# Moving one of nine small start-up transfers from ScalarE's DMA queue to the sync engine's

## The chip, the cores and the metric

The kernel runs on one core of a Trainium2 chip. The metric is the device time of one execution in microseconds (us). Before the change the median of 8 executions is 555.18 us (554.63 to 556.37). The engines are PE (TensorE: matmuls; PEld is its weight load), ACT (ScalarE), DVE (VectorE), POOL (GpSimd) and SP (the sync engine, which issues DMAs only). ACT can issue DMAs as well; "ACTq" and "SPq" in the profile are such issues.

## The reference, cut to what matters

Two layers, each an attention with a compressive memory followed by a feed-forward part, on 2048 tokens of width 640, with 32 heads of width 20. The sequence is cut into four segments of 512 tokens; within a segment attention is causal softmax, and across segments a memory matrix built from a feature map of the keys is read by the mapped queries.

```
phi = lambda t: jnp.where(t > 0, t + 1.0, jnp.exp(t))
for s in range(N):
    qs, ks, vs = (q[:, :, s].copy(), k[:, :, s].copy(), v[:, :, s].copy())
    logits = jnp.einsum('bhqd,bhkd->bhqk', qs, ks) * scale + mask
    p = _softmax(logits, axis=-1)
    a_dot = jnp.einsum('bhqk,bhkd->bhqd', p, vs)
    pq = phi(qs)
    num = jnp.einsum('bhld,bhde->bhle', pq, M)
    den = jnp.einsum('bhld,bhd->bhl', pq, z)[..., None] + 1e-06
    o = g * (num / den) + (1.0 - g) * a_dot
    pk = phi(ks)
    M = M + jnp.einsum('bhld,bhle->bhde', pk, vs)
    z = z + jnp.einsum('bhld->bhd', pk)
...
x = x + _A_ref(_layernorm(x, axis=-1), A_wq, A_wk, A_wv, A_wo, A_beta)
x = x + _B_ref(_layernorm(x, axis=-1), B_w1, B_w2)
```

The last two lines run twice, with the same weights.

## The kernel before

The program is not written in its final order. Some forty Python generators ("streams") each describe one kind of work: scores, exponentials, causal masks, projections, layer norms, spills to DRAM, fills from DRAM, the feed-forward part, and so on. A greedy planner (`Sched.run`, line 295) asks every stream for its next instruction, works out from hand-written costs when that could start on each engine that may take it, picks the one with the smallest start time (ties go to the smaller priority number), appends it to that engine's list and moves the engine's clock to its end. A stream that waits for an event which no other stream has set yet (`Need`) offers nothing. So the planner's clocks decide the order of all 18,665 instructions, and the chip then runs each engine's list in order, with semaphore waits between them.

The costs that matter here are in the helpers. `act` (line 404) charges 60 ns + n/1.2 for n columns read from PSUM, 94 ns + n/1.2 for others; `dve` (line 399) charges 66 ns + n/(0.96 x mode). `evac` (line 408), an evacuation from PSUM to SBUF, offers both ACT and DVE and takes the one that the planner believes to end first. `dma` (line 417) charges the issuing engine's clock with `issue` and gives a landing time from size and `lat`.

The heads are worked on in pairs of groups: a group is 4 heads (80 rows of the 640 features), and a pair is 8 heads. For the score matmuls, each head's 20 rows of queries and keys must stand at partition 0, 32, 64 or 96 of a buffer called `pad`. The projections leave queries and keys in `stg`, in 5 chunks of 128 feature rows. For all pairs but the first, a chunk goes out to DRAM (`spill`, line 942; its DMA is line 955) and comes back in the padded layout (`fill`, line 989; line 1002), all on SP. For the very first pair of segment 0 the detour is left out: `first_heads` (line 960) copies straight from `stg` to `pad`, one DMA for each head (line 982), z = 0 being the first group and z = 1 the second, hh = 0 to 3 the head in the group. The third head of the second group straddles the border of chunks 0 and 1 and is moved in two pieces (8 and 12 rows). So z = 0 makes 4 DMAs, all on SP, and z = 1 makes 5, all on ACT. Each is planned with `issue=720.0`.

When the last piece of a group is planned, `first_heads` sets the event `pad` of that group. At the end it sets `direct` 0 and 1. Three streams hang on these:

- the scores (`scores`, line 1164; the matmuls are line 1186). A pair goes through five rounds; rounds 0 and 1 read only group z = 0, rounds 2 to 4 read z = 1. The exponentials (line 1248, ACT) follow round by round, two for each.
- `spill` of chunk 1 in segment 0 starts with `Need("direct", 1)`, though its DMA waits only for the evacuations of chunk 1. Chunk 0 isn't spilled; its event `packed` is set with the tickets of `direct` 0, that is with the landing of the last piece of both groups.
- the feature map (`phi_`, line 1010) of a chunk waits for `packed`: DVE line 1029, then ACT line 1031, then DVE line 1032, priority 4.

Other names that the text uses: line 621 loads beta on SP (in `consts`, priority 7), and ACT's line 624 waits for it; line 550 are SP's loads of later tokens (`late_loads`, priority 8); line 734 (DVE) normalises the next segment's tokens (`lnorm`, priority 5), line 710 transposes them by DMA, and the projections of that segment follow (lines 667 and 670 are the two ways in which `group` emits a matmul: whole, or as four of 32 columns; the planner chooses by the mode that PE is in, and charges a change of mode). Lines 866 and 867 are the evacuations of queries and keys on DVE and ACT; line 921 is the evacuation of values on either.

Of the kernel before, what the change touches and what calls it, by code (L numbers as in the profile page):

```python
# [38 lines left out]
class Prog:  # L39
# [44 lines left out]
    def dma(self, e, fn, sem):  # L84
        self.pos[e] += 1
        self.dcnt[id(sem)] = self.dcnt.get(id(sem), 0) + 16
        tk = (sem, self.dcnt[id(sem)])
        self.ops[e].append(("op", fn, sem, 16))
        self.info[(id(sem), tk[1])] = ("dma%d" % id(sem), tk[1], dict(self.K[e]))
        return tk  # L90
# [332 lines left out]
def bass_interleave_layers__memory_aug_infini_attn__dense_activation_relu__prompt_kernel(  # L423
    nc, A_x, A_wq, A_wk, A_wv, A_wo, A_beta, B_x, B_w1, B_w2, out,
):
    with contextlib.ExitStack() as es:
# [533 lines left out]
        def first_heads():  # L960

            sl = yield Acq(PAD)
            sems = pad_sem[id(sl)], sem_("first")
            tks = []
            for z in range(2):
                ev = []
                for n in range(2):
                    t = yield Need("stg", 0, 0, 0, n)
                    ev = ev + t
                sem = sems[z]  # L970
                for hh in range(4):
                    r0 = 80 * z + 20 * hh
                    cuts = [r0, r0 + DH] if r0 // 128 == (r0 + DH - 1) // 128 else [r0, 128, r0 + DH]
                    for ra, rb in zip(cuts, cuts[1:]):
                        c = ra // 128
                        if c == 1 and ra == 128:
                            ev = []
                            for n in range(2):
                                t = yield Need("stg", 0, 0, 1, n)
                                ev = ev + t  # L980
                        p0 = 32 * hh + ra - r0
                        tk = yield dma(("sp", "act")[z], sem, 2048 * (rb - ra), lambda e, p0=p0, ra=ra, rb=rb, c=c, z=z: e.dma_start(  # L982
                            sl.ap[p0:p0 + rb - ra, z], stg[ra - 128 * c:rb - 128 * c, c]), ev + sl.tks, issue=720.0, rate=200.0)
                S.set("pad", 0, 0, z, tks=[sl, tk])
                tks.append(tk)
            S.set("direct", 0, tks=tks)
            S.set("direct", 1, tks=tks[1:])

        def fill(a, s):
            got = []  # L990
            for g in range(0, G, 2):
                if (a, s, g) == (0, 0, 0):
                    yield from first_heads()
                    continue
                sl = yield Acq(PAD)
                w = []
                for c in range(80 * g // 128, (80 * g + 159) // 128 + 1):
                    t = yield Need("packed", a, s, c)
                    w += t
                for hh in range(4):  # L1000
                    src = scr[s % 2, 80 * g:80 * g + 160, :].rearrange("(g h d) t -> d h g t", g=2, d=DH)[:, hh]
                    tk = yield dma("sp", pad_sem[id(sl)], 81920, lambda e, sl=sl, src=src, hh=hh: e.dma_start(  # L1002
                        sl.ap[32 * hh:32 * hh + DH].rearrange("p g n t -> p g (n t)"), src), w + sl.tks, issue=350.0, rate=130.0)
                for z in range(2):
                    S.set("pad", a, s, g + z, tks=[sl, tk])
                got.append(tk)
            S.set("filled", a, s, tks=got)
# [622 lines left out]
```

The softmax here doesn't subtract the row's maximum and nothing guards it: scores larger than these inputs give would overflow.

## Time and profile before

| what | value |
|---|---|
| median of 8 executions | 555.18 us (554.63 to 556.37) |
| the profiled execution, its own time | 555.04 us |
| its span, first to last instruction | 553.3 us |
| granted TensorE clock | 1.000 |
| exponentials, ACT line 1248 | 320, 308.9 us, mean 1027 ns |
| evacuation of 512 columns, ACT line 867 / DVE line 866 | mean 598 / 684 ns |
| evacuation of 320 columns, ACT line 921 / DVE line 921 | mean 441 / 485 ns |
| line 982 on SP | 4, median 718 ns, 13.2 to 15.7 us |
| line 982 on ACT | 5, median 732 ns, 14.6 to 19.3 us |
| beta load, line 621, issue to landing | 2.8 us |

The profile is one execution of the whole program. Times in it run from the first instruction. "Busy" of an engine excludes DMA issues, which the profile shows as the engine's queue. A wait of several semaphores is put down to the one that came last. The difference of 1.7 us between the execution's time and its span lies before the first and after the last instruction.

### The profile page before, as it was taken

To read this page: it belongs to the slowest core of one execution; us is meant where nothing else is said; L and a number is where in the kernel's file an instruction comes from. 1 tells how busy PE (TensorE), PEld (TensorE's weight loads), DVE (VectorE), ACT (ScalarE), POOL (GpSimd) and SP (SyncE) were. 2 spreads that over 40 slices of the span, in tenths; PEclk is the share of its full clock that TensorE was granted. 3 is DMA by queue.
4 is the path that set the end of the run, shared out by engine and by line. 5 is a ranking of instruction groups with operands and counts; after the bars stand their busy time and mean duration, and the time that the engine had idled before them with its cause. 6 is when DMAs were issued, how large, how long until landed. Compare 5 with 4: busy or idle time off the path is not lost.

```text
span 553.3 us, 18665 instructions
## 1 busy us (share of the span) xinstructions
PE 545.1 (99%) x8130; PEld 309.0 (56%) x8130; DVE 412.1 (74%) x1061; ACT 407.3 (74%) x516; POOL 189.7 (34%) x302
## 2 busy tenths in 40 slices
PE   8999999999999999999999999999999999999998
PEld 7454554455564555646456554565555654666756
DVE  5967989898799888897878888769885787335102
ACT  5699889889777987798788887679987678432140
POOL 5346344333344344343433443035331443201000
DMA  8596999935845148256186521872429512354101
GB/s 273 134 235 159 233 181 212 231 65 70 191 92 91 31 101 189 50 98 88 39 184 127 88 45 39 166 153 39 69 61 208 103 30 30 87 84 62 40 2 51
DMA packets 130291, 61.30 MB, mean 111 GB/s; under 512 B 109090, under 2 KB 120098, under 8 KB 130210
## 3 DMA queue, kind: packets, MB, share of 16 engines
q1 hardware_dynamic: 129648, 59.58, 50.7%
q8 instruction: 64, 1.05, 0.8%
q10 hardware_dynamic: 562, 0.53, 0.3%
q14 instruction: 17, 0.14, 0.1%
HBM read 20.57 MB, written 12.85 MB: 60 GB/s over the span
## 4 chain that ended last, share of the span: by engine, by line
PE 94%; ACT 2%; DMA 1%; DVE 1%; SPq 1%; issue 0%; POOL 0%; ACTq 0%; POOLq 0%
PE ps L667 47%; PE ps L670 25%; PE ps L1186 9%; PE ps L1280 6%; PE ps L1066 2%; PE ps L1319 1%; ACT PT L1248 1%; PE ps L1123 1%; PE ps L644 1%; PE ps L1460 1%; DMA pad<-scr 1%; DMA beta_bc<-in_A_beta_dram 1%; SPq L982 0%; ACT stg L867 0%; SPq L1002 0%
## 5 line engine op out<-in xcount | busy, mean ns | idle before, releaser
L1248 ACT ACTIVATE PT<-ps 128x1024 bf16<-128x1024 f32 x320 | 308.9, 1027 | 65.5 <-PE ps L1186 60.1
L1260 POOL TENSOR_SCALAR_AFFINE_SELECT PT<-PT 128x512 bf16<-128x512 bf16 x256 | 163.8, 658 | 264.3 <-ACT PT L1248 264.2
L667 PE MATMUL ps<-w_r,hT 128*128 128x320 bf16 x510 | 82.4, 300 | 0.0
L1506 DVE TENSOR_TENSOR x_sb<-x_sb,ps 128x320 bf16<-128x320 bf16 (+1 forms) x65 | 31.1, 478 | 59.5 <-PE ps L670 44.2
L670 PE MATMUL ps<-xnT,w_r 128*32 128x512 bf16 x1112 | 65.4, 379 | 0.3 <-issue 0.3
L1186 PE MATMUL ps<-pad 20*128 20x512 bf16 (+3 forms) x1024 | 63.4, 301 | 1.5 <-ACT PT L1248 0.9
L667 PEld LDWEIGHTS ps<-w_r,hT 128*128 128x128 bf16 x510 | 47.6, 98 | 24.5 <-issue 6.8
L667 PE MATMUL ps<-xnT,w_r 128*128 128x512 bf16 x242 | 59.8, 380 | 0.0
L688 DVE BATCH_NORM_STATS2 stats<-x_sb 128x6 f32<-128x320 bf16 x124 | 55.8, 474 | 2.6 <-DMA x_sb<-in_A_x_dram 2.2
L1485 ACT ACTIVATE hT<-ps 128x512 bf16<-128x512 f32 x56 | 33.5, 598 | 21.8 <-PE ps L670 20.5
L670 PE MATMUL ps<-w_r,hT 128*32 128x320 bf16 (+1 forms) x1340 | 49.0, 294 | 0.0
L1186 PEld LDWEIGHTS ps<-pad 20*128 20x128 bf16 x1024 | 17.8, 92 | 52.6 <-ACT PT L1248 28.1
L1402 DVE TENSOR_TENSOR x_sb<-x_sb,ps 128x320 bf16<-128x320 bf16 x64 | 30.0, 480 | 18.1 <-PE ps L667 10.2
L670 PEld LDWEIGHTS ps<-xnT,w_r 128*32 128x32 bf16 x1112 | 29.1, 97 | 25.2 <-issue 0.6
L1280 PE MATMUL ps<-PT,v_aug 128*21 128x128 bf16 (+3 forms) x896 | 40.4, 301 | 0.0
L670 PEld LDWEIGHTS ps<-w_r,hT 128*32 128x32 bf16 x1340 | 34.8, 97 | 9.0
L667 PE MATMUL ps<-wo_r,oT 128*128 128x320 bf16 x242 | 38.9, 300 | 0.0
L1290 DVE CAST otu<-ps 128x512 bf16<-128x512 f32 x48 | 32.8, 682 | 7.5 <-PE ps L1280 6.9
L1484 DVE TENSOR_SCALAR hT<-ps 128x512 bf16<-128x512 f32 x48 | 32.7, 682 | 6.4 <-PE ps L667 4.3
L704 POOL TENSOR_TENSOR rstd<-lnU,mhalf 128x2 f32<-128x2 f32 (+2 forms) x26 | 20.6, 791 | 46.0 <-DVE lnU L700 36.1
L667 PEld LDWEIGHTS ps<-xnT,w_r 128*128 128x128 bf16 x242 | 21.7, 97 | 24.5 <-issue 4.6
L866 DVE CAST stg<-ps 128x512 bf16<-128x512 f32 x45 | 30.6, 684 | 5.8 <-PE ps L667 5.6
(109 smaller groups left out, 735.8 us busy)
## 6 DMA issues: line engine op xcount, KB each, us to landing
pad<-scr SPq DMA_DIRECT2D x124, 80.0 KB
scr<-stg SPq DMA_DIRECT2D x34, 256.0 KB, 3.1
out_dram<-x_sb SPq DMA_DIRECT2D x15, 160.0 KB, 1.8
w_r<-in_B_w_dram SPq DMA_DIRECT2D x10, 216.0 KB, 2.6
w_r<-in_B_w_dram SPq DMA_DIRECT2D x13, 160.0 KB, 3.0
x_sb<-in_A_x_dram SPq DMA_DIRECT2D x10, 160.0 KB, 3.3
scr<-w_r SPq DMA_DIRECT2D x5, 256.0 KB, 3.0
wv_r<-in_A_wv_dram SPq DMA_DIRECT2D x1, 800.0 KB, 8.5
```

The costliest lines, as they stand in the source:

```text
L667: return e.matmul(view(dst.ap, b), a, b, start=(k == 0), stop=(k == last))
L670: return e.matmul(view(dst.ap[rows], b), part, b, start=(k == 0), stop=(k == last))
L688: tk = yield dve(320, 1, lambda e, c2=c2: e.bn_stats(stats6[:, t % 12, c2, :], x_sb[:, t, c2 * 320:(c2 + 1) * 320]), xt)
L866: te = yield evac(N, 1, lambda e: e.tensor_copy(sg.ap[:, t0:t0 + N], bk.ap[:, 0:N]), lambda e: e.activation(sg.ap[:, t0:t0 + N], bk.ap[:, ...
L1186: fns.append([(lambda e, z=z, j=j, hh=hh, N=N, o=o, sl=sl, q=hh % 2: e.matmul(slot.ap[:, q, o:o + N], sl.ap[32 * hh:32 * hh + DH, z, 0, 12 ...
L1248: tx = yield act(1024, lambda e, dst=dst, src=src: e.activation(dst, src, ACT.Exp, scale=SCALE), sc + pw)
L1260: tm = yield pool(600.0, lambda e, reg=reg: e.affine_select(out=reg, in_=reg, pattern=[[0, 4], [1, 128]], compare_op=ALU.is_ge, fill=0.0, ...
L1280: fns.append((lambda e, OD, j=j, hh=hh: e.matmul(OD.ap[32 * hh:32 * hh + DH + 1, 128 * j:L], VAUG[vx(a, s)][:, j, 4 * g + hh, :], pt.ap[:, ...
L1290: te = yield evac(L, 1, lambda e: e.tensor_copy(dst, OD.ap), lambda e: e.activation(dst, OD.ap, ACT.Copy), [tk] + OTU[0].tks)
L1484: th = yield evac(512, 1, lambda e: e.tensor_scalar(hT[:, dc, :], bk.ap[:, :], 0.0, None, ALU.max), lambda e: e.activation(hT[:, dc, :], b ...
L1485: lambda e: e.activation(hT[:, dc, :], bk.ap[:, :], ACT.Relu), [tk] + HT.tks)
L1506: ta = yield dve(n, 1, lambda e: e.tensor_tensor(x_sb[:, t, c0:c0 + n], x_sb[:, t, c0:c0 + n], bk.ap[:, 0:n], ALU.add), [tk], urgent=True)
```

## The change

The DMA of the fourth head of the second group (z = 1, hh = 3; 20 rows of 2048 bytes) is issued by SP. The other four pieces of z = 1 stay on ACT. The semaphore, the data and the planned cost are the same.

```diff
                         p0 = 32 * hh + ra - r0
-                        tk = yield dma(("sp", "act")[z], sem, 2048 * (rb - ra), lambda e, p0=p0, ra=ra, rb=rb, c=c, z=z: e.dma_start(
+                        tk = yield dma("act" if z and hh < 3 else "sp", sem, 2048 * (rb - ra), lambda e, p0=p0, ra=ra, rb=rb, c=c, z=z: e.dma_start(
                             sl.ap[p0:p0 + rb - ra, z], stg[ra - 128 * c:rb - 128 * c, c]), ev + sl.tks, issue=720.0, rate=200.0)
```

## The prediction, made before the changed kernel was run

> **What bounds the kernel now.** I read the busy times and the chain that ended last, then stretches of 20 us, then the queues around the change.
>
> ```profile
> PE 545.1 (99%) x8130; PEld 309.0 (56%) x8130; DVE 412.1 (74%) x1061; ACT 407.3 (74%) x516; POOL 189.7 (34%) x302
> PE 94%; ACT 2%; DMA 1%; DVE 1%; SPq 1%; issue 0%; POOL 0%; ACTq 0%; POOLq 0%
> ```
>
> TensorE (PE) is busy for 545.1 of 553.3 us, so 8.2 us is all the time in which it does nothing. The stretches show where those lie (columns: length, PE, PE weight load, DVE, ACT, POOL, clock, DMA share, GB/s):
>
> ```profile
> 0.00:20.00 20.00, 17.62 (x154) 13.86 (x155) 12.41 (x37) 9.89 (x23) 7.32 (x23) 1.00 0.67 204
> 20.00:40.00 20.00, 19.38 (x226) 10.12 (x224) 15.98 (x41) 19.13 (x25) 9.30 (x15) 1.00 0.90 227
> 40.00:60.00 20.00, 18.61 (x310) 9.97 (x311) 16.35 (x46) 19.99 (x22) 11.63 (x18) 1.00 0.70 175
> 60.00:80.00 20.00, 20.00 (x230) 11.86 (x232) 17.23 (x51) 16.03 (x25) 6.61 (x10) 1.00 0.96 213
> 80.00:100.00 20.00, 19.47 (x321) 8.59 (x313) 17.82 (x46) 18.71 (x25) 8.40 (x13) 1.00 0.84 193
> ```
>
> Before 20 us PE lacks 2.38 us, the start-up. From 20 to 60 it lacks 0.62 + 1.39 = 2.01 us, and there ACT works 19.13 and then 19.99 of 20 us: this is the stage in which ACT, not PE, sets the pace. From 80 to 100 PE lacks 0.53. All stretches from 100 to 540 together lack 0.74 (0.08 at 200, 0.18 at 320, 0.46 at 340, 0.02 at 420), and the last, short one 2.54, the end chain. Outside start and end that makes 2.01 + 0.53 + 0.74 = 3.28 us. Elsewhere PE is the limit, and only another order of its work, or work it must wait for, changes the end.
>
> Now ACT and then SP around the change, in order of time (start, length, engine or its queue, line):
>
> ```profile
> 16.75 0.67 ACTq L982 DMA_DIRECT2D pad<-stg  x1
> 17.48 0.73 ACTq L982 DMA_DIRECT2D pad<-stg  x1
> 19.30 0.23 ACT L624 ACTIVATE gt<-beta_bc 128x32 f32<-128x32 bf16 x1 [1.24 <-DMA beta_bc<-in_A_beta_dram]
> 19.31 0.73 ACTq L982 DMA_DIRECT2D pad<-stg  x1
> 19.44 1.01 ACT L1248 ACTIVATE PT<-ps 128x1024 bf16<-128x1024 f32 x1
> 20.34 1.02 ACT L1248 ACTIVATE PT<-ps 128x1024 bf16<-128x1024 f32 x1
> 21.85 1.02 ACT L1248 ACTIVATE PT<-ps 128x1024 bf16<-128x1024 f32 x1 [0.49 <-PE ps L1186]
> ```
>
> ```profile
> 15.70 0.71 SPq L982 DMA_DIRECT2D pad<-stg  x1
> 16.45 0.49 SPq L621 DMA_DIRECT2D beta_bc<-in_A_beta_dram  x1
> 20.47 0.82 SPq L550 DMA_DIRECT2D x_sb<-in_A_x_dram  x2
> 21.34 0.43 SPq L955 DMA_DIRECT2D scr<-stg  x1
> ```
>
> The reader is to see three things. The piece that moves is the last of ACT's five, issued at 19.31. While ACT's queue issues it, ACT's datapath runs two exponentials without a gap, from 19.44 to 20.34 + 1.02 = 21.36. And SP issues nothing between 16.45 + 0.49 = 16.94 and 20.47.
>
> **The change part by part.** One DMA of 20 partitions x 2048 bytes leaves ACT's queue and enters SP's; nothing else is added or removed.
>
> *What leaves ACT.* 1 issue x 0.73 us. It lies wholly under the two exponentials; the next one starts at 21.85 and waits for scores (line 1186), which themselves wait for the second exponential. So it is worth 0 here. Had it no cover, it would be worth the whole 0.73: bounds -0.73 to 0, value 0.
>
> *What enters SP.* 1 issue x 0.72 us (median of SP's own four on line 982; 0.71 to 0.91). The generator hands the pieces out one after another, and the fourth ACT piece is issued at 17.48, when SP's beta load (16.45) is already out; so the planner should put the moved piece behind that load, into SP's gap of 20.47 - 16.94 = 3.53 us, and 2.8 us of the gap remain. Its sources are ready (chunk 1 is evacuated by 13.90 + 0.38 = 14.28), so it blocks nobody. Cost 0. If it came ahead of the beta load instead, that load, the ACT instruction of line 624 that sits waiting for it, and the first exponential behind that in ACT's queue would all be 0.72 later: bounds 0 to +0.72, value 0.
>
> *What lands earlier.* SP's last piece of the first group was issued at 15.70 and the scores that need it start at 18.02, so a piece takes about 2.32 us from issue. The moved one lands at about 16.94 + 2.32 = 19.26 rather than 19.31 + 2.32 = 21.63. The first scores that read it are the round that starts at 24.01 and waits for exponentials, so nothing is gained there.
>
> [...]
>
> *What the earlier event sets free.* Two streams wait in the planner for this piece. The spill of chunk 1 (line 955, now at 21.34) cannot be planned before it; with the change it can follow at 16.94 + 0.72 = 17.66, some 3.7 us sooner. The feature map of chunk 0 waits for its landing: DVE line 1029 (0.28 us, now at 23.46), ACT line 1031 (0.64, now at 23.99), DVE line 1032 (0.41). Its priority 4 beats the normalisation (5), so it can go ahead of that. On ACT the 0.64 can use the 0.49 us gap before 21.85: at best -0.49. On DVE 0.28 + 0.41 = 0.69 us comes ahead of the next segment's normalisation (line 734, from 22.12), which feeds the transposes at 23.34 and the projections that PE runs from 28.40: at worst +0.69. Net of the two: +0.20.
>
> *What is planned again.* The program is a greedy list: each step takes the instruction that the planner believes can start first. ACT's clock in it loses 720 ns of work at the place where evacuations choose between ACT and DVE by the earlier end, and one different choice alters which buffer is free first, and so the order behind it. I expect the order to differ from about 20 us to the end. The trace of before can't show the new order's waits. Nearest rows: the 3.28 us that PE lacks now. If the new order had none of it, -3.28; if it had twice as much, +3.28. I take half of the upper bound, +1.64, because of what the planner's costs leave out. It charges ACT 60 ns + n/1.2, 913 ns for an exponential that takes 1027, 487 for an evacuation of 512 that takes 598, 327 for one of 320 that takes 441; for DVE it charges 599 and 399 against 684 and 485. Each ACT step is thus underrated by 111 to 114 ns, each DVE step by about 85. An ACT that looks 0.72 us freer receives evacuations and feature maps that DVE did, in the very stage where ACT has 0.01 us idle in 20. After the 0.49 us gap is filled, each costs 0.44 to 0.60 us of exponentials; three or four of them are the 1.64.
>
> *Sum.* 0 + 0 + 0.20 + 1.64 = +1.84. The profiled execution took 555.04 us (553.3 of span and 1.7 around it), which makes 556.9; from the median 555.18 it would be 557.0. I say 556.9, with 556.3 to 559.7 as this case's own range: the upper end takes all upper bounds, 0.72 + 0.69 + 3.28 = 4.69.
>
> **The rivals.** *Faster: the early feature map pays.* Place: 20 to 60 us. With chunks 0 and 1 mapped in gaps that ACT has before 21.85, 0.49 us of ACT work is gone from the stage where ACT is full, and PE's 2.01 us of waits there shrink; later the new order also loses waits. It decides if ACT gets no more evacuations in that stage than now. For it: the gap is there, and SP's is too. Against: DVE has none between 22.1 and 26 us. Price: -0.49 - 1.64 (half of what PE lacks) = -2.13, so 552.9; all of it and the 0.73 would be -4.50, 550.5.
>
> *No difference: the transfer is hidden anyway.* The direct effects are 0, and from 60 us on PE runs at 20.00 of 20 whatever the order, because projections and feed-forward fill every wait. Time 555.2, or 555.9 if the piece gets ahead of the beta load. Against: only the fillers' amount is fixed, not their place, and a stage short of fillers (340 to 360 lacks 0.46) may become another's. The variant that the change doesn't do what it says (the list comes out as before but for the queue) belongs here; the choice of ACT or DVE that follows speaks against it.
>
> **How the numbers follow.** This kernel's measurement can tell about 0.2%, 1.1 us, from no change. Forecast (slower) 0.50, faster rival 0.30, no difference 0.20. The forecast's bounds reach over 556.3, the faster rival's below 554.1; so slower 0.50, same 0.20, faster 0.30. The range goes from 552.4, a little below the faster rival's 552.9, to 559.7; about 0.12 is left below and 0.06 above.
>
> **What would show it.** Right: in the changed trace ACT issues four pieces of line 982 and SP five, the fifth between the beta load and the loads of line 550; the spill of line 955 is issued before 19 us; line 1029 starts before 23; ACT's exponentials keep 19.44; from 20 to 60 us PE lacks more than 2.01 us, and ACT has more instructions besides its exponentials. Wrong: PE lacks less there, or the loss lies past 60 us in waits that have nothing to do with ACT, or PE's own work (count and mode of its matmuls) differs by more than its waits do.

## The result and the profile after

The changed kernel took 558.49 us (median of 11 executions, 557.61 to 559.78); the kernel before, run beside it, 555.33 (32 executions, 554.19 to 557.47). The ratio is 1.0055 [1.0043, 1.0067]: slower by about 3.1 us, beyond the 0.2% that can be told from no change. The profiled execution of the changed kernel took 557.07 us (span 555.0), the lowest of all of them; a second one, taken later, took 559.18 (span 557.1). Both have a granted clock of 1.000, and where it matters I give both. In every execution of the changed kernel 2.0 to 2.2 us of the time lie outside the span; in the kernel before it is 1.7 to 1.9. So about 0.3 of the 3.1 us lies before the first instruction or after the last, and no run here says why.

First the busy times and the chain that ended last, of the changed kernel.

```profile
PE 546.2 (98%) x8136; PEld 306.5 (55%) x8136; DVE 413.0 (74%) x1063; ACT 406.3 (73%) x514; POOL 190.3 (34%) x302
...
PE 88%; DVE 4%; ACT 3%; DMA 2%; SPq 1%; issue 0%; POOL 0%
```

PE is busy as before to within 1.1 us, but its share of the chain fell from 94 to 88%, and DVE (from 1 to 4%), ACT (2 to 3%) and DMA (1 to 2%) have taken over: somewhere PE now waits for a path that runs through these. The stretches of 20 us show where (length, PE, PE weight load, DVE, ACT, POOL, clock, DMA share, GB/s).

```profile
0.00:20.00 20.00, 17.39 (x155) 13.44 (x156) 12.54 (x38) 9.99 (x23) 7.22 (x23) 1.00 0.71 219
20.00:40.00 20.00, 19.15 (x225) 9.98 (x222) 16.54 (x43) 19.55 (x26) 9.27 (x14) 1.00 0.85 207
40.00:60.00 20.00, 18.56 (x309) 9.82 (x309) 16.23 (x45) 19.99 (x23) 11.65 (x18) 1.00 0.72 180
60.00:80.00 20.00, 19.48 (x187) 11.87 (x188) 15.69 (x47) 15.32 (x24) 5.84 (x9) 1.00 0.99 206
80.00:100.00 20.00, 19.55 (x272) 8.32 (x268) 17.99 (x43) 18.16 (x23) 8.91 (x14) 1.00 0.95 179
100.00:120.00 20.00, 19.45 (x259) 9.11 (x248) 17.53 (x50) 17.73 (x24) 7.68 (x12) 1.00 0.72 174
```

From 20 to 60 us PE lacks 0.85 + 1.44 = 2.29 us where it lacked 2.01: hardly a change. From 60 to 120 it lacks 0.52 + 0.45 + 0.55 = 1.52 us where it lacked 0.53. After 120 us it lacks nothing but the end, where the kernel before lacked 0.74 up to 540 us; over the whole span its idle time is 555.0 - 546.2 = 8.8 us, 0.6 more than before. So the new waits lie between 60 and 120 us, not in the stage in which ACT is full.

Now the place of the change: ACT and its queue, then SP's queue (start, length, engine or queue, line).

```profile
17.35 0.73 ACTq L982 DMA_DIRECT2D pad<-stg  x1
19.20 0.23 ACT L624 ACTIVATE gt<-beta_bc 128x32 f32<-128x32 bf16 x1 [1.26 <-DMA beta_bc<-in_A_beta_dram]
19.34 1.92 ACT L1248 ACTIVATE PT<-ps 128x1024 bf16<-128x1024 f32 x2
21.14 0.63 ACT L1031 ACTIVATE stg<-stg 128x512 bf16<-128x512 bf16 x1
```

```profile
16.33 0.48 SPq L621 DMA_DIRECT2D beta_bc<-in_A_beta_dram  x1
16.87 0.73 SPq L982 DMA_DIRECT2D pad<-stg  x1
17.64 0.55 SPq L955 DMA_DIRECT2D scr<-stg  x1
20.37 0.81 SPq L550 DMA_DIRECT2D x_sb<-in_A_x_dram  x2
```

The piece stands on SP behind the beta load, the spill of chunk 1 follows at 17.64, the first exponential starts at 19.34 (19.44 before), and the gap that ACT had before its third exponential now holds a feature map (line 1031 at 21.14). All of this is as forecast, and none of it is late. The delay comes 40 us further on, and three views show how it gets there.

*The feature map is one chunk further.* Line 1032 on DVE ends the map of a chunk. In the kernel before, three maps came early (the third at 29.53) and the fourth only when the segment's exponentials were done, at 61.17; in the changed kernel the fourth slips in at 32.83, 28 us earlier. The two views show line 1032 on DVE, before and then after.

```profile
29.53 0.43 DVE L1032 TENSOR_TENSOR phs<-stg,rtmp 128x512 bf16<-128x512 bf16 x1
...
61.17 0.69 DVE L1032 TENSOR_TENSOR phs<-stg,rtmp 128x512 bf16<-128x512 bf16 x1
...
62.85 0.40 DVE L1032 TENSOR_TENSOR phs<-stg,rtmp 128x512 bf16<-128x512 bf16 x1
```

```profile
28.54 0.41 DVE L1032 TENSOR_TENSOR phs<-stg,rtmp 128x512 bf16<-128x512 bf16 x1
...
32.83 0.62 DVE L1032 TENSOR_TENSOR phs<-stg,rtmp 128x512 bf16<-128x512 bf16 x1 [0.77 <-ACT stg L1031]
...
61.38 0.69 DVE L1032 TENSOR_TENSOR phs<-stg,rtmp 128x512 bf16<-128x512 bf16 x1
```

*So the transposition of the mapped keys is ready sooner, and takes SP's queue.* The mapped keys of chunks 3 and 4 are transposed by one DMA (line 710, `phk`) for the second part of the memory write (line 1123). The fifth map ends at 61.38 + 0.69 = 62.07 instead of 62.85 + 0.40 = 63.25, and SP's queue shows what follows, before and then after. Line 1002 is the fill that brings the next segment's queries and keys to `pad`.

```profile
61.97 2.19 SPq L1002 DMA_DIRECT2D pad<-scr  x6
64.20 3.31 SPq L710 DMA_TRANSPOSE oT<-o_sb  x2
67.56 0.89 SPq L1002 DMA_DIRECT2D pad<-scr  x2
...
69.76 3.38 SPq L710 DMA_TRANSPOSE phk<-phs  x2
```

```profile
62.09 1.23 SPq L710 DMA_TRANSPOSE phk<-phs  x1
63.45 2.65 SPq L1002 DMA_DIRECT2D pad<-scr  x4
66.14 3.00 SPq L710 DMA_TRANSPOSE oT<-o_sb  x2
69.18 1.93 SPq L1002 DMA_DIRECT2D pad<-scr  x4
```

Before, six fills went out from 61.97 and both transpositions of `phk` came last, at 69.76. After, one of them stands first, and the first fill goes out at 63.45, 1.48 us later.

*The next segment's scores wait for that fill.* PE's scores (line 1186) and memory writes, before and then after:

```profile
67.04 0.39 PE L1186 MATMUL ps<-pad 20*128 20x512 bf16 x4
...
78.07 0.29 PE L1123 MATMUL ps<-w_r,phk 128*128 128x147 bf16 x2
```

```profile
66.55 0.68 PE L1123 MATMUL ps<-w_r,phk 128*128 128x147 bf16 x8
...
68.94 0.39 PE L1186 MATMUL ps<-pad 20*128 20x512 bf16 x4 [0.39 <-DMA pad<-scr]
```

The wait that the profile puts down to the fill is only 0.39 us, but the scores are 1.90 us later, because the memory write has come in front of them and PE has filled the rest with other work. ACT sees it whole: between the start of the last exponential of one segment and that of the first of the next lay 67.47 - 59.28 = 8.19 us, and now 69.38 - 59.48 = 9.90. The chain of waits of the changed kernel, from 63 to 69 us, goes through just these pieces (start, length, what):

```profile
63.15 0.18 SPq L710
...
63.45 1.38 SPq L1002
...
65.76 3.13 DMA pad<-scr
...
68.94 0.39 PE ps L1186 x4
```

In the kernel before, the same stretch of the chain is PE without a break.

The fill's 0.39 us is not the largest wait of PE between 60 and 120 us. That one comes at 113.63, where scores wait 0.55 us for an exponential (another 0.18 us of this kind comes at 82.30):

```profile
113.63 0.40 PE L1186 MATMUL ps<-pad 20*128 20x384 bf16 x8 [0.55 <-ACT PT L1248]
```

The chain shows why that exponential is late: in ACT's list a feature map of the next segment stands before it (line 1031), and that waits for DVE (line 1029), at the end of a run of DVE work that begins with a transposed DMA at 101.73.

```profile
110.44 0.65 DVE rtmp L1029
...
111.12 0.63 ACT stg L1031
111.75 1.83 ACT PT L1248 x2
```

The kernel before has neither of these two waits, the 0.39 us for the fill and the 0.55 us for the exponential; its one wait for an exponential from 60 to 120 us is 0.2 us. That the second follows from the first, through everything that the late scores move, is argued here and not shown. The exponentials catch up later (the last one starts at 476.88, against 476.67); I put that down to feed-forward work that PE brings forward while it waits for them, and what it could not fill stays as time at the end.

### The profile page after: what moved, and what is told of

The parts are those of the page before. It is cut to its first block, busy times and chain, and to the rows that moved or that the text cites. A ratio compares the mean times of both kernels' runs of the same rounds, so it can differ in the third digit from the quotient of the medians.

```text
span 555.0 us, 18662 instructions
## 1 busy us (share of the span) xinstructions
PE 546.2 (98%) x8136; PEld 306.5 (55%) x8136; DVE 413.0 (74%) x1063; ACT 406.3 (73%) x514; POOL 190.3 (34%) x302
## 4 chain that ended last, share of the span: by engine, by line
PE 88%; DVE 4%; ACT 3%; DMA 2%; SPq 1%; issue 0%; POOL 0%
PE ps L667 43%; PE ps L670 26%; PE ps L1186 9%; PE ps L1280 6%; ACT PT L1248 3%; PE ps L1066 1%; PE ps L1123 1%; PE ps L1460 1%; DVE stats L688 1%; PE ps L1319 1%; DMA otk<-otu 1%; DMA pad<-scr 1%; DMA x_sb<-in_A_x_dram 1%; DMA beta_bc<-in_A_beta_dram 1%; SPq L982 0%; DVE w_r L866 0%
## 5 line engine op out<-in xcount | busy, mean ns | idle before, releaser
L667 PE MATMUL ps<-w_r,hT 128*128 128x320 bf16 x475 | 77.5, 300 | 0.0
L667 PE MATMUL ps<-xnT,w_r 128*128 128x512 bf16 x273 | 67.0, 380 | 0.0
L670 PE MATMUL ps<-xnT,w_r 128*32 128x512 bf16 x988 | 58.3, 379 | 0.0
L667 PEld LDWEIGHTS ps<-w_r,hT 128*128 128x128 bf16 x475 | 43.7, 98 | 22.5 <-issue 6.8
L670 PE MATMUL ps<-w_r,hT 128*32 128x320 bf16 (+1 forms) x1480 | 54.5, 294 | 0.0
L1485 ACT ACTIVATE hT<-ps 128x512 bf16<-128x512 f32 x62 | 37.1, 599 | 21.9 <-PE ps L670 20.9
L670 PEld LDWEIGHTS ps<-w_r,hT 128*32 128x32 bf16 x1480 | 37.7, 97 | 11.3
L667 PEld LDWEIGHTS ps<-xnT,w_r 128*128 128x128 bf16 x273 | 24.5, 98 | 28.6 <-issue 4.8
L670 PEld LDWEIGHTS ps<-xnT,w_r 128*32 128x32 bf16 x988 | 25.5, 97 | 22.5 <-DVE om_sb L1081 0.2
L1031 ACT ACTIVATE stg<-stg 128x512 bf16<-128x512 bf16 x50 | 31.7, 634 | 5.0 <-DVE rtmp L1029 5.0
```

The lines of the kernel that those rows point to most:

```text
L667: return e.matmul(view(dst.ap, b), a, b, start=(k == 0), stop=(k == last))
L670: return e.matmul(view(dst.ap[rows], b), part, b, start=(k == 0), stop=(k == last))
L1031: te = yield act(512, lambda e, q=q: e.activation(q, q, ACT.Exp), [tr] + p, psum=False)
L1485: lambda e: e.activation(hT[:, dc, :], bk.ap[:, :], ACT.Relu), [tk] + HT.tks)
```

## The experiments

An experiment on a greedy planner has to change one thing and leave its other picks alone. For the first three, each pick was recorded (engine, waits, instructions), the list was edited, and the semaphores were worked out again from the edited list, so that every other engine's order stays exactly as it was. The others change a condition in a stream and let the planner plan again.

**1. The queue alone** (the order of the kernel before on every engine; only the last piece leaves ACT's list and stands in SP's, behind the beta load).

```diff
+    at = [r[3] is piece for r in rec].index(True)
+    r = rec.pop(at)
+    prev = max(n for n in range(at) if rec[n][3].dma is r[3].dma)
+    rec.insert(prev + 1, ["sp"] + r[1:])
```

> Every engine keeps the order of before; only the last piece leaves ACT's list and stands in SP's, right behind the beta load. Theory (the new order of the program costs the 3.1 us): 555.3, within 0.5 us of before, with the first exponential at 19.4 and the fifth SP piece near 16.9. Rival (the queue itself costs, by SP's issue of 0.73 us or by the earlier landing): most of the 3.1 us, so 557.5 or more. Rival (ACT's freed 0.73 us is worth something by itself): 554.6.

Measured: 1.001 [0.9993, 1.0026], 557.11 us against 556.05 of the kernel before beside it. The medians lie 1.06 us apart, more than the 0.5 expected, but four of the twelve executions, and three of the other 23, have a lower clock (0.997; see the last section); without those the medians are 556.44 and 556.04. So no difference that can be told: at most 0.26%, 1.4 us, less than half of the loss.

**2. The order alone** (the order of the changed kernel; the piece is issued by ACT again).

```diff
+    at = [r[3] is piece for r in rec].index(True)
+    rec[at][0] = "act"
```

> Every engine keeps the order of the changed kernel, but the last piece is issued by ACT, behind its fourth piece and ahead of line 624, where ACT waits for the beta load anyway. Theory (the order costs): 558.5, that is 3 us over before. Rival (the queue costs): 555.3 to 556.

Measured: 1.0053 [1.0034, 1.0073], 558.86 us. The order, with the piece on its old queue, costs what the change costs. The intervals of runs 1 and 2 don't meet: the loss is the planner's, not the transfer's.

**3. SP's list alone** (the changed kernel; the four fills are put before the transposition of `phk` in SP's list, PE's list stays).

```diff
+    ...
+    k = [n for n in sp if line(n) == 710][5]
+    f = [n for n in sp if n > k and line(n) == 1002][:4]
+    rec.insert(f[3], rec.pop(k))
```

> The changed kernel with one exchange in SP's list: the four fills (line 1002) of the first pair of segment 1 go ahead of the 128x8x128 transpose of the mapped keys (line 710) that stands before them and waits until 62.1 us. If that new wait (the scores at 68.9 wait for the fills; PE lacks 0.52 us between 66 and 70, the 40th exponential is 1.9 us late) is what costs most: 556.5 to 557.2, and PE lacks nothing from 66 to 70. If the loss is spread over the whole order, and projections fill that wait anyway: 558.0 to 558.5.

Measured: 1.0062 [1.0044, 1.008], 559.6 us, where 556.5 to 557.2 was expected if the fill's wait cost most. PE in this kernel:

```profile
67.70 0.69 PE L1123 MATMUL ps<-w_r,phk 128*128 128x147 bf16 x8 [1.43 <-DMA phk<-phs]
...
69.65 0.39 PE L1186 MATMUL ps<-pad 20*128 20x512 bf16 x4
```

The fill is in time now, but the memory write still stands ahead of the scores in PE's list, and waits 1.43 us for the transposition that was put back. The wait changed its name, not its place.

**4. The early spill alone** (the kernel before, but the spill of chunk 1 doesn't wait in the planner for the last piece; the map's wait for its landing stays).

```diff
-                    direct = yield Need("direct", c)
...
-                S.set("packed", a, s, c, tks=[tk] + direct)
+                S.set("packed", a, s, c, tks=[tk] + ((yield Need("direct", 1)) if (a, s, c) == (0, 0, 1) else []))
```

> The planner of before, all nine pieces where they were (four on SP, five on ACT, each charged 720), but the spill of chunk 1 may be planned without waiting for the last piece (only its event still waits). So of the three things that the change did to the plan (ACT's clock, the spill's place, the early feature map) this does one. Theory (any new order moves the time by some us, whichever way the list falls): a time that differs from 555.3 by 0.5 to 4 us, direction not known. Rival (the earlier spill is what brings the bad order): 558 or more. Rival (the earlier spill is harmless, ACT's clock does it): 555.3 within 0.5.

Measured: 1.004 [1.0025, 1.0055], 558.33 us. Slower too, but by another way: SP issues this spill ahead of the beta load (16.29 and 16.81), six fills go out ahead of the transpositions of `phk` (64.47 and 72.74), and the memory write is not early (80.43). In the profiled execution ACT is busy for only 2.65 of 4 us from 28 us on and 3.07 from 32 on (4.00 and 3.68 in the kernel before), but that execution has a granted clock of 0.64 and then 0.93 in these two stretches, which by itself is up to an estimated 0.36 x 4 + 0.07 x 4 = 1.7 us, so where this plan loses isn't shown. It shows that this order is easily lost, and says nothing of the route above.

**5. The clock alone** (the kernel before; the piece stays on ACT, but the planner charges ACT nothing for it).

```diff
+   ... issue=720.0 if z * hh < 3 else 0.0 ...
```

> Nothing moves to SP: the last piece stays on ACT, but the planner charges ACT's clock nothing for it, so it is planned early (ahead of the first exponentials), and the spill and the feature map follow early as in the change. SP's clock isn't charged either. Theory (what the planner does with ACT's freed 0.72 us and the early event is the cause, not SP): slower than before by 0.3% or more, 557 to 565. Rival (SP's issue is needed for the loss): 555.3 within 0.5.

Measured: 1.0088 [1.0066, 1.011], 561.5 us. No piece has moved to SP here, so a change of the planner's clock, with the earlier event that follows from it, is enough to lose time. But it loses more than the change does, with yet another order: four fills (62.69) and the scores (68.58) stand ahead of the transposition (65.85) and the memory write (70.30).

**6. The transposition later** (the changed kernel; the second transposition of segment 0's mapped keys isn't planned before the first fill of segment 1). The early feature maps stay.

```diff
                 w = yield Need("phk", a, s, p)
-                yield Acq([PHK[p]])
+                w = w + (((yield Need("pad", 0, 1, 0)) and []) if (a, s, p) == (0, 0, 1) else []); yield Acq([PHK[p]])
```

> The changed kernel, planned again with one constraint: the 128x8x128 transpose of segment 0's mapped keys may be planned only after the first fill of segment 1. SP's list between 54 and 72 us is then that of before again (six fills, then the transposes of o, then those of the keys), and the second part of segment 0's memory write goes back from 66 to about 78 us on PE. Theory (the earlier feature map pulls this memory write, with its transpose, into the stretch from 58 to 70 us where the fills need SP; that is what costs): 555.0 to 556.5, PE full from 60 to 80 and from 100 to 120. Rival (any order other than before's costs 2 to 3 us, wherever): 557.5 or more.

Measured: 1.0012 [0.9996, 1.0028], 556.84 us, against 556.34 of the kernel before beside it (555.0 to 556.5 was expected): the loss is gone but for what can't be told from nothing. SP's queue of this kernel, in the place shown above:

```profile
62.58 3.46 SPq L1002 DMA_DIRECT2D pad<-scr  x6
66.09 3.02 SPq L710 DMA_TRANSPOSE oT<-o_sb  x2
69.15 1.17 SPq L1002 DMA_DIRECT2D pad<-scr  x2
...
71.22 3.86 SPq L710 DMA_TRANSPOSE phk<-phs  x2
```

The fills are first again, the memory write is back at 78.68, and the exponentials' gap is 68.09 - 59.75 = 8.34 us. The stretches from 60 us on, of this kernel:

```profile
60.00:80.00 20.00, 19.93 (x222) 11.88 (x223) 15.38 (x48) 16.18 (x25) 6.60 (x10) 1.00 0.83 202
80.00:100.00 20.00, 19.44 (x337) 8.61 (x321) 17.68 (x45) 18.68 (x25) 8.29 (x12) 1.00 0.91 202
100.00:120.00 20.00, 20.00 (x226) 9.91 (x219) 17.58 (x50) 17.48 (x22) 7.84 (x12) 1.00 0.66 158
```

PE lacks 0.07 + 0.56 = 0.63 us here, as before (0.53), and not 1.52. From 20 to 60 us it lacks 2.32, with the fourth map at 33.10, as in the changed kernel. So the early maps themselves cost no more than can be told here; what they set free does. About 0.3 us of what is left lies outside the span, as in the changed kernel. The rival "any other order than the one before costs half a per cent" falls: this order differs, and doesn't.

**7. The first map later** (the changed kernel; the map of chunk 0 held until the third round of scores).

```diff
-                    p = yield Need("packed", a, s, c)
+                    p = (yield Need("packed", a, s, c)) + (((yield Need("sc", 0, 2, 0)) and []) if (a, s, c, n) == (0, 0, 0, 0) else [])
```

> The changed kernel, planned again, but the feature map of chunk 0 may be planned only after the first pair's third round of scores, about where it stood before. The spill of chunk 1 and ACT's freed clock stay. Theory of the early map: the transpose of the mapped keys stays late and the time is 555 to 556.5. Rival (any other order costs): 557.5 or more. The list of SP still has that transpose ahead of the fill, so a loss as in the changed kernel would say that holding back chunk 0 alone isn't enough.

Measured: 1.0151 [1.0126, 1.0176], 564.81 us. Worse. In this order the transposition of `phk` (63.89) and two others are all issued ahead of the fills, which go out at 68.49. It agrees with the route in direction, but loses time elsewhere too (PE 17.77 of 20 from 160 to 180), so it measures nothing by itself.

**8 and 9. More, and another, piece on SP**: all five pieces of the group, and then the first head's piece in place of the last's.

```diff
+   "sp"                               # all five; the first argument of `dma`, the rest cut
+   "act" if z and hh > 0 else "sp"    # the first only
```

> All five pieces of the second group go to SP: five times the dose. Were there a price for each piece on SP (rival, queue): 5 x 0.73 us on SP ahead of the beta load, which ACT waits for, and 5 x 3.1 = 15 us at the most, 560 or more. Theory (the order decides, by chance rather than by dose): within 555 to 560, no proportion to the number of pieces.

> Another single piece (the first head of the second group, not the last) goes to SP. The same dose as the change: 0.73 us off ACT's planned clock, one more issue on SP. Rival (queue, or ACT's clock alone): the same 558.5. Theory (the order decides): a different time, 554 to 560.

Measured: 1.0157 [1.0131, 1.0182] (565.26 us) and 1.0204 [1.0177, 1.0232] (568.03 us), both beyond the 555 to 560 and 554 to 560 expected. Part of it is the clock: all four executions of each have a lower one, 0.994 to 0.997 and 0.988 to 0.994. An estimate takes (1 - clock) x span off every execution: the medians are then 562.8 and 562.6 us against 556.1 for the kernel before, 1.2% each. So one piece of the same size costs half a per cent or over one by which one it is, and five cost no more than the dearer one. The cost has no proportion to what is moved.

**10 and 11. The changed kernel and the mended one on the same chip.** The first is the changed kernel once more; the second holds the transposition back until an exponential of segment 1 rather than until the fill, and comes out as the same program as run 6.

```diff
+   w = w + (((yield Need("ex", 4, 0)) and []) if (a, s, p) == (0, 0, 1) else [])
```

> The changed kernel itself, so that the next ones stand beside it on one chip. All theories: about 1.0055 of before, 558.5 where before is 555.4.

> The transpose of segment 0's mapped keys may be planned only after the fifth pair's first exponentials instead of after the first fill of segment 1; the program comes out as in e6_turn_later, instruction for instruction, so this repeats that run beside the changed kernel. Theory: within 0.2% of before, 0.3 to 0.5% under the changed kernel of this call. If e6_turn_later was a good chip or a good day: with the changed kernel.

Measured: 1.005 [1.0033, 1.0066] (559.2 us) and 1.0012 [0.9994, 1.003] (557.24 us). The intervals don't meet. The condition is worth 0.0050 - 0.0012 = 0.0038, or 2.1 us, of 2.8. Among executions with a clock of 0.999 or more the medians are 559.2, 557.1 and, for the kernel before, 555.9 us: the condition takes 2.1 of 3.3 us back, and 1.2 stay. In the profiled execution of the changed kernel of this pair the stretches are:

```profile
60.00:80.00 20.00, 19.41 (x194) 12.02 (x191) 15.62 (x46) 15.75 (x25) 5.39 (x8) 1.00 1.04 211
80.00:100.00 20.00, 19.10 (x234) 7.96 (x231) 17.34 (x44) 17.71 (x23) 9.29 (x14) 1.00 0.92 171
100.00:120.00 20.00, 18.96 (x275) 8.87 (x275) 16.73 (x49) 16.64 (x21) 6.68 (x11) 1.00 0.70 186
```

PE lacks 0.59 + 0.90 + 1.04 = 2.53 us from 60 to 120 here, 2.00 more than the kernel before, and 2.37 from 20 to 60, 0.36 more. Waits for the fill are 0.39 of it, for the transposition 0.20, for exponentials 0.73, for DVE 0.65 and for nothing that the profile shows 0.56. This execution's time, 559.18, is near the median; the first profile's was the lowest of its kernel, and it showed a smaller loss.

**12. The memory write alone** (the changed kernel; only PE's half is held back: the second part of the memory write isn't planned before an exponential of segment 1; the transposition keeps its early place on SP).

```diff
-                    pht = yield Need("phkT", a, s, p)
+                    pht = (yield Need("phkT", a, s, p)) + (((yield Need("ex", 4, 2)) and []) if (a, s, p) == (0, 0, 1) else [])
```

> The changed kernel, planned again with only the second part of segment 0's memory write held back on PE (until the fifth pair's third round of exponentials is planned); its transpose stays ahead of the fill in SP's list. It parts the two halves of the theory. If PE's own wait for the transpose is the costly half: 555.5 to 557. If the transpose in SP's list, which delays the fill of the next scores by 1.3 us or more, is the costly half: 557.5 to 559. If a plan other than before's costs by chance: anything up to 565.

Measured: 1.0046 [1.0028, 1.0064], 559.05 us. The memory write is at 76.81, out of the way, and yet:

```profile
69.20 0.40 PE L1186 MATMUL ps<-pad 20*128 20x512 bf16 x4 [0.92 <-DMA pad<-scr]
```

SP's queue is as in the changed kernel (transposition at 62.08, fills at 63.43), and the wait for the fill has grown from 0.39 to 0.92 us: the memory write had only covered it. This 0.92 us isn't the whole of its loss: from 60 to 120 us PE lacks 0.92 + 1.31 + 1.26 = 3.49 us, and its longest wait of the whole execution for an exponential is 1.2 us. With run 3 this tells the two halves apart at that place. With SP's half undone PE waits for the transposition, with PE's half undone it waits for the fill; neither alone takes the loss away, and most of it goes when both go (run 6).

What stays open. Runs 6 and 12 let the planner plan everything behind the condition again, so the 2.1 us belong to the plan with that condition; an order in which only SP's and PE's lists are exchanged at that place was not tried. Of the eight orders that were planned anew (the changed kernel's and those of runs 4 to 9 and 12) only run 6's comes within noise of the kernel before, and runs 4, 5 and 9 lose with their fills ahead of that transposition, so that run 6 is one lucky order among eight isn't ruled out. The 0.12% left in run 6 can't be told from nothing. And of the 3.8 us by which the second profile's span is longer than that of before (557.1 - 553.3), 1.7 us are time in which PE does nothing; the other 2.1 lie within its busy time, in no one group of matmuls. (The first profile of the same program has 1.0 us less busy time, so half of this is what two executions differ by.) The mix of whole matmuls and of those split in four differs (for the group of 320 columns, 475 and 1480 against 510 and 1340), but that group as a whole takes 132.0 us against 131.4.

## Why the prediction was right, and where it was not

The forecast case (slower) came true, and the time, 558.5, lies in its own range. By steps:

- *What leaves ACT, valued 0.* Right. The first exponential didn't move, and run 1 has the issue off ACT at 1.001 with an interval that holds 1 and ends at 1.0026.
- *What enters SP, valued 0.* Right, with its place: the issue was forecast for 16.94 and came at 16.87, and the beta load kept its place ahead of it.
- *What lands earlier, no gain for the scores.* Right as far as it shows: line 1029, which waits for the piece to land, starts at 20.46, which fits the landing estimated at 19.26. For the transfer itself the sum of 0 holds within the 1.4 us that run 1 can tell.
- *What the earlier event sets free, valued +0.20.* The events came as said: the spill at 17.64 (forecast 17.66), line 1029 at 20.46, line 1031 in ACT's gap at 21.14. **This is the mis-sized term.** I followed the early map to the normalisation that it might delay, and stopped there. Its further effect, the transposition that becomes ready at 62.07 and is planned ahead of the fills, is worth about 2.1 us, as far as the new plan of runs 6 and 11 shows it. The 0.20 itself may well be right: run 6 keeps the early maps, and PE lacks 0.31 us more there from 20 to 60.
- *What is planned again, valued +1.64.* The order does differ from 20 us to the end, and runs 1 and 2 show that the loss is the order's. **But the reason for the sum failed**: I put it down to three or four evacuations that an underrated ACT would take over from 20 to 60 us. There ACT has 49 instructions for 47 and 39.54 us of work for 39.12, with three evacuations as before and one map more, and PE lacks 0.28 to 0.36 us more, a fifth of 1.64. That half of PE's idle time was near the measured loss is luck of size, not of cause, and so is the direction as far as it rested on this term.
- *The signs.* All that were named for "right" appeared, the last two (more than 2.01 us lacking from 20 to 60, and more instructions on ACT besides its exponentials, 7 for 6 before) barely. Of those named for "wrong", one appeared in part: the loss lies past 60 us, some of it in waits for a fill, a transposition and DVE; but 0.73 of the 1.52 us that PE lacks from 60 to 120 are waits for exponentials on ACT. Another appeared in full: PE's busy time grew by more than its idle time, 1.1 us for 0.6 in the first profile and 2.1 for 1.7 in the second. So the direction and the range were right and the mechanism, placed between 20 and 60 us, was wrong.
- *The rivals.* "Faster" had the right first step, a free map in ACT's gap; what it left out is that earlier work isn't better when it stands in a queue ahead of something urgent, as the transposition at 62.09 does ahead of the fill. "No difference" was right for the transfer alone, and that is run 1.

## What to carry to other kernels

When a transfer changes its queue in a kernel that a planner orders, cost the transfer and the order apart: replaying the recorded order with only the queue changed gave 1.001, and the planner's new order on the old queue 1.0053. Follow an event that comes earlier to the next queue that is served in order, and ask what stands behind the work that it sets free there; here the bill came 40 us later and, as far as the replanned runs show, most of it from a transposition whose result the old order read only at 78 us, issued at 62 ahead of a fill that the next scores were waiting for. A fix that moves one of two linked waits is no test of their cause until the other has been moved too.

## What the runs showed of the hardware that was not expected

In the kernel before, ACT's queue issued a DMA beside running activations: the issue at 19.31 (0.73 us) lay beside exponentials that ran from 19.44 to 21.36 without a gap. There the moved issue cost ACT nothing, and on SP (16.87, in the changed kernel) it stood in a gap; run 1 finds no difference between the two.

The same program differs from one execution to the next by about as much as the change costs (the kernel before: 554.19 to 557.47 us), and one part of it is the granted clock. Runs 6 and 11 are one program; their profiled executions took 556.58 and 559.33 us. From 56 to 60 us they show, run 6 and then run 11:

```profile
56.00:60.00 4.00, 4.00 (x64) 2.07 (x63) 4.00 (x10) 4.00 (x6) 2.49 (x4) 1.00 1.01 232
```

```profile
56.00:60.00 4.00, 3.96 (x13) 1.14 (x14) 3.22 (x7) 3.28 (x4) 2.35 (x5) 0.57 0.97 223
```

The mean granted clock was 0.57 over these 4 us, and 1.00 from 60 to 62. An estimate from this is a loss of (1 - 0.57) x 4 = 1.7 us, and the scores that start at 67.66 in run 6 start at 69.44, 1.78 us later, in run 11. In run 1 the clock was 0.71 from 56 to 58 us, 0.50 from 58 to 60 and 0.94 from 60 to 62, by the same sum 0.58 + 1.00 + 0.12 = 1.7 us. It comes to 1.7 us too in run 2 (0.98 from 52 to 56, 0.59 from 56 to 60), run 4 (0.64 from 28 to 32, 0.93 from 32 to 36), run 5 (0.58 from 96 to 100) and run 8 (0.72 from 168 to 172, 0.85 from 172 to 176), and twice in run 9 (0.85 from 60 to 64 and 0.73 from 64 to 68; 0.57 from 100 to 104). The profiled executions of the kernel before, of the changed one (both) and of runs 3, 6, 7 and 12 have a mean clock of 1.000. What makes the clock fall is not shown by any run.

At 1.7 us, more than half of the effect looked for, one profile can mislead: PE's lack in run 2's stretches can't be set against that of the first profile of the changed kernel, and the verdicts above rest on the medians of four to twelve executions. The changed kernel's loss is not of this kind: all eight executions of run 10 have a clock of 0.999 or more.
